# Attention inside the first MoE: transposes one unit later, and the sinks of all heads in one go

## The chip, the cores and the metric

The kernel runs on one core of a Trainium2 chip. The metric is the device time of one execution in microseconds (us). Engines are named as the profile names them: PE (matrix products; PEld is its weight loading), DVE, ACT and POOL (element-wise work), SP (issues transfers).

## The reference

```python
scores = scale * np.matmul(q, k.transpose(0, 1, 3, 2))
keep = is_sink | in_window                     # 4 sink columns, window 128
scores = np.where(keep, scores, -1000000000.0)
a = np.exp(scores - np.max(scores, axis=-1, keepdims=True))
a = a / (np.sum(a, axis=-1, keepdims=True) + 1e-09)
attn_out = np.matmul(a, v)                     # (4, 8, 768, 64)
x = attn_out.transpose(0, 2, 1, 3).reshape(B * S, H * D)   # 3072 x 512
return (x @ w_a) * (x @ w_b) @ w_out           # w_a, w_b: 512 x 1536, w_out: 1536 x 512
```

The window and the number of sinks are inputs, but this kernel has a fast path for 128 and 4.

## The kernel before

The 3072 rows are 24 tiles of 128 rows (6 of each of 4 batches). They are processed in groups. The first group is tile 0 of every batch. While PE works at the MoE of one group (12 blocks j; of each a products with w_a, b products with w_b, and o products that project the block before), the attention of the next group is woven into it: `moe` calls `between` three times a block, and each call takes as many steps of a generator as are due. The first such attention, here the second attention of the kernel, is that of batch 0, tiles 1 and 2, and lies between about 30 and 147 us of the span. It is written by `first_attention`, `parts_exact` and `pipeline`. It has 16 units (h, i): 8 heads by 2 tiles, and takes 21 steps.

A unit does this. `scores` (L732) makes s on PE; DVE adds the mask (L736); ACT takes the exponential (L738); DVE makes the reciprocal of the sum (L740, L741); ACT scales (L742). `transposes` (L757) turns p on PE, two 128x128 blocks, and ACT copies them into `ptx` (L758). After an odd head, `av` (L769) makes eight calls of products for the pair of heads, and ACT copies the result into `xf` (L771). Tile 2 sees the sinks apart from its window. Its four sink columns are kept by POOL (L747); for each pair of heads `sinks_t` turns them (L777), DVE copies them (L779), `sinks_av` multiplies them with the v of the sinks (L784), and DVE adds that to `xf` (L786). In this text t(6,0) means the transposes of head 6, tile 0, s(7,1) the scores of head 7, tile 1, av(2) the av of the third pair of heads, which fills `xf` number 2, and sinks product 2 that of the same pair.

All transposes and products of this attention use one PSUM tile, which `half_bank` hands out in two halves, the first for transposes, the second for av and the products of sinks:

```python
bank[0] = self.ps.tile([P, 4, P], F32, tag="t", name=name)
return bank[0][:, 2:] if second else bank[0][:, :2]
```

Beside this attention DVE and ACT also split the weights of the MoE into a high and a low part (L336, L337, L348, L360, L366), DVE multiplies a and b into g (L889), ACT rounds it to gh (L892), and POOL makes the first q and k of the group after (L387, L390). When the generator is through, `split_x` splits `xf` into xh (ACT, L829) and xl (DVE, L830), four parts (kk) of 128 columns of x each, for the next MoE, whose products need all four. Its blocks are called a128, b128 and o128. The order of the instructions on each engine is made by a scheduler in the compilation; the code above gives it only the order of priority.

Of the kernel before, what the change touches and what calls it, by code (L numbers as in the profile page):

```python
# [19 lines left out]
P = 128  # L20
# [209 lines left out]
class Fast:  # L230
# [326 lines left out]
    def first_attention(self, segs, xf, after):  # L557
        (_, t0, nt), = segs
        late = [i for i in range(nt) if t0 + i >= 2]
        units = [(h, i) for h in range(H) for i in range(nt)]  # L560
        return self.pipeline(units, nt, late, *self.parts_exact(*segs[0], xf, after), 2, 2, 1)

# [122 lines left out]
    def parts_exact(self, b, t0, nt, xf, after):  # L685
# [17 lines left out]
        def do_prep(h):  # L703
# [8 lines left out]
            if h % 2 == 0:  # L712
                v = self.sp.tile([P, 2, MB, D], F32, tag="v", name=f"vx{u}")
                nc.sync.dma_start(v[:, :, :nb], self.vB[b, h // 2, :, :, s0:s0 + nb])
            else:
                v = preps[h - 1][2]
                if late:
                    vs = ptx[:2 * NS, h // 2 % 2, 2 * nt + 1, :]
                    m = h // 2
                    nc.sync.dma_start(vs, self.vS[b, m * 2 * NS:(m + 1) * 2 * NS, m])  # L720
                    vss[h // 2] = vs
            preps[h] = k, q, v

        def scores(h, i):
# [19 lines left out]
            if i in late:  # L744
                if h % 2 == 0:
                    sc[h // 2, i] = self.at.tile([P, 2, NS], F32, tag=f"sc{i % 3}", name=f"sc{u}", bufs=2)
                nc.gpsimd.tensor_copy(sc[h // 2, i][:, h % 2, :], p[:, P:P + NS])  # L747

# [23 lines left out]

        def sinks_t(pr):
            n = len(late)
            tp = half_bank(0, f"skt{tag}_{pr}")
            for k, i in enumerate(late):
                nc.tensor.transpose(tp[:2 * NS, k, :], sc[pr, i].rearrange("p a b -> p (a b)"), self.ident)  # L777
            skt[pr] = ptx[:2 * NS, pr % 2, 2 * nt:2 * nt + n, :]
            nc.vector.tensor_copy(skt[pr], tp[:2 * NS, :n, :])  # L779

        def sinks_av(pr, _):
            n = len(late)
            ps = half_bank(1, f"sk{tag}_{pr}")
            nc.tensor.matmul(ps[:, :n, :], lhsT=vss[pr], rhs=skt.pop(pr), start=True, stop=True)  # L784
            xs = xf[pr][:, late[0] * P:nt * P].rearrange("p (c q) -> p c q", q=P)
            nc.vector.tensor_tensor(xs, ps[:, :n, :], xs, op=ALU.add)  # L786

        return do_prep, scores, transposes, av, sinks_t, sinks_av

    def pipeline(self, units, nt, late, do_prep, scores, transposes, av, sinks_t, sinks_av, lag, group, early):  # L790

        for h in range(early):
            do_prep(h)
        yield
        nu = len(units)
        for k in range(nu + lag + 2 + group // 2):
            if k < nu:
                h, i = units[k]
                if i == 0:
                    do_prep(h + early)  # L800
                scores(h, i)
            n = k - lag - 1
            if 0 <= n < nu and units[n][1] == nt - 1:
                h = units[n][0]
                av(h)
                if h % group == group - 1 and late:
                    sinks_t(h // group)
            for c in range(group // 2):
                n -= 1
                if 0 <= n < nu and units[n][1] == nt - 1:  # L810
                    h = units[n][0]
                    if h % group == group - 1 and late:
                        sinks_av(h // group, c)
            n = k - lag
            if 0 <= n < nu:
                transposes(*units[n])
            yield


# [251 lines left out]
```

## Time and profile before

| what | value |
|---|---|
| median of 3 runs | 757.04 us (756.62 to 757.09) |
| the profiled execution, own time | 756.8 us |
| its span (first to last instruction) | 755.1 us |
| granted clock of PE, mean | 0.999 of full speed |

The span is the time that the trace covers. The 1.7 us between it and the execution's own time lie around it.

### The profile page before, as it was taken

The page shows a single profiled execution, that of the slowest core. Times are in us where ns is not written, and L with a number is a line of the kernel's source. Part 1 is how long each engine was busy: PE and PEld are TensorE (multiplying, and loading weights), DVE is VectorE, ACT ScalarE, POOL GpSimd, SP SyncE. Part 2 cuts the span into 40 slices and gives each one's busy share as a digit, 9 for nine tenths or more (in the row PEclk, how much of TensorE's full clock was granted, in tenths as well). Part 3 has the DMA queues.
Part 4 walks back from the last instruction along what each step waited for, and adds up shares of the span by engine and source line. Part 5 has one row for each costly group of instructions (what it writes and reads, how often), then busy time and mean ns, then how long its engine had stood idle before and what let it go on. Part 6 is the DMA issues. An engine that isn't in the chain of part 4 may idle for free.

```text
span 755.1 us, 13078 instructions
## 1 busy us (share of the span) xinstructions
PE 745.2 (99%) x4422; PEld 665.7 (88%) x4422; DVE 389.8 (52%) x1303; ACT 387.4 (51%) x1185; POOL 275.5 (36%) x358
## 2 busy tenths in 40 slices
PE   8999999999999999999999999999999999999996
PEld 6877777889899998999989999899989999999996
DVE  6899998455455553445544554355553555331001
ACT  6777765466455663555535555355554655331111
POOL 2200021176425542355404545056561764201110
PEclk9999999999999999999999999999999999999999
DMA  9997111322213343124422344124443141010001
GB/s 333 394 318 279 33 40 40 118 72 75 64 46 85 105 141 92 57 85 123 132 82 70 96 126 138 63 75 124 115 121 114 47 132 47 2 42 1 1 1 44
DMA packets 48807, 76.89 MB, mean 102 GB/s; under 512 B 5056, under 2 KB 28640, under 8 KB 48736
## 3 DMA queue, kind: packets, MB, share of 16 engines
q1 hardware_dynamic: 45568, 70.50, 29.6%
q10 hardware_dynamic: 3168, 5.51, 1.9%
q8 instruction: 36, 0.59, 0.3%
q14 instruction: 35, 0.29, 0.1%
HBM read 69.70 MB, written 6.29 MB: 101 GB/s over the span
## 4 chain that ended last, share of the span: by engine, by line
PE 90%; DMA 3%; DVE 3%; ACT 1%; POOL 1%; issue 1%; SPq 0%; DVEq 0%; POOLq 0%; ACTq 0%
PE a L846 26%; PE o L873 25%; PE b L846 25%; PE s L628 5%; PE av L659 5%; PE t L648 2%; DMA raw_a<-in_wa_dram 1%; DMA raw_o<-in_wo_dram 1%; DMA v<-in_v_dram 1%; PE sk L679 1%; PE s L732 1%; DMA qr<-in_qT_dram 1%; PE t L757 0%; PE t L769 0%; DVE wf_o L348 0%
## 5 line engine op out<-in xcount | busy, mean ns | idle before, releaser
L846 PE MATMUL a<-xh,w_a 128*128 128x384 f32 (+2 forms) x760 | 212.3, 342 | 0.1
L846 PE MATMUL b<-xh,w_b 128*128 128x384 f32 (+2 forms) x760 | 209.9, 340 | 0.5 <-DVE w_b L366 0.5
L873 PE MATMUL o<-w_o,gh 128*128 128x512 f32 x576 | 182.4, 398 | 0.0
L894 POOL TENSOR_TENSOR gl<-g,gh 128x384 fp32r<-128x384 f32 (+1 forms) x70 | 68.2, 974 | 225.9 <-ACT gh L892 221.6
L846 PEld LDWEIGHTS a<-xh,w_a 128*128 128x128 f32 x760 | 137.2, 188 | 8.3 <-issue 1.7
L846 PEld LDWEIGHTS b<-xh,w_b 128*128 128x128 f32 x760 | 137.2, 188 | 5.8 <-issue 1.0
L846 PE MATMUL a<-xl,w_a 128*128 128x384 f32 (+2 forms) x380 | 127.8, 336 | 0.0
L846 PE MATMUL b<-xl,w_b 128*128 128x384 f32 (+2 forms) x380 | 127.7, 336 | 0.0
L873 PEld LDWEIGHTS o<-w_o,gh 128*128 128x128 f32 x576 | 103.9, 188 | 18.8 <-issue 0.9
L873 PE MATMUL o<-w_o,gl 128*128 128x512 f32 x288 | 113.3, 394 | 0.0
L889 DVE TENSOR_TENSOR g<-b,g 128x384 f32<-128x384 f32 (+2 forms) x95 | 52.8, 555 | 112.6 <-PE b L846 111.5
L636 ACT ACTIVATE p<-p,st 128x132 f32<-128x132 f32 x144 | 58.0, 403 | 74.4 <-DVE st L634 73.2
L892 ACT CAST gh<-g 128x384 fp32r<-128x384 f32 (+2 forms) x96 | 49.3, 513 | 88.6 <-DVE g L889 88.6
L883 ACT COPY g<-a 128x384 f32<-128x384 f32 (+2 forms) x95 | 45.0, 474 | 91.2 <-PE a L846 85.7
L633 DVE COPY_PREDICATED s<-own,s 128x128 f32<-128x128 uint16 x144 | 42.0, 291 | 82.0 <-PE s L628 80.4
L846 PEld LDWEIGHTS a<-xl,w_a 128*128 128x128 f32 x380 | 71.4, 188 | 2.7
L639 ACT ACTIVATE p<-p,st 128x132 f32<-128x132 f32 x144 | 58.2, 404 | 29.3 <-DVE st L638 28.6
L846 PEld LDWEIGHTS b<-xl,w_b 128*128 128x128 f32 x380 | 71.4, 188 | 1.7
L390 POOL TENSOR_TENSOR ks<-kr,ks 64x524 fp32r<-64x524 f32 (+1 forms) x64 | 70.4, 1110 | 3.9
L873 PEld LDWEIGHTS o<-w_o,gl 128*128 128x128 f32 x288 | 54.1, 188 | 12.9 <-DVE gl L894 0.9
L637 DVE TENSOR_SCALAR st<-st 128x1 f32<-128x1 f32 x144 | 21.9, 152 | 74.8 <-ACT p L636 74.8
L387 POOL TENSOR_SCALAR qh<-qr 128x384 fp32r<-128x384 f32 x48 | 24.9, 519 | 86.4 <-DMA qr<-in_qT_dram 49.4
(166 smaller groups left out, 1029.7 us busy)
## 6 DMA issues: line engine op xcount, KB each, us to landing
raw_a<-in_wa_dram SPq DMA_DIRECT2D x12, 512.0 KB, 7.8
raw_b<-in_wb_dram SPq DMA_DIRECT2D x12, 512.0 KB, 6.3
raw_o<-in_wo_dram SPq DMA_DIRECT2D x12, 512.0 KB, 6.9
qr<-in_qT_dram SPq DMA_DIRECT2D x32, 192.0 KB, 2.6
chk_a<-in_wa_dram SPq DMA_DIRECT2D x24, 256.0 KB, 3.2
chk_b<-in_wb_dram SPq DMA_DIRECT2D x24, 256.0 KB, 3.0
chk_o<-in_wo_dram SPq DMA_DIRECT2D x24, 256.0 KB, 3.1
out_dram<-os ACTq DMA_DIRECT2D x21, 256.0 KB, 2.1
```

The lines of the kernel that those rows point to most:

```text
L390: self.nc.gpsimd.tensor_tensor(o, i, high.bitcast(F32), op=ALU.subtract)
L628: nc.tensor.matmul(ps, lhsT=q[:, i * P:(i + 1) * P], rhs=ks[:, c0s[i]:c0s[i] + SW], start=n == 0, stop=n == 1)
L633: nc.vector.copy_predicated(ps[:, :P], self.own.bitcast(mybir.dt.uint16), ps[:, W:])
L636: nc.scalar.activation(p, p, AF.Exp, bias=st[:, 0:1], scale=-1.0, accum_out=st[:, 1:2])
L639: nc.scalar.mul(p, p, st[:, 3:4])
L659: nc.tensor.matmul(ps[half[e], c * P:(c + ns) * P], lhsT=v[:, e, blk, :], rhs=pt[:, e, sl:sl + ns, :], start=j == 0, stop=j == len(groups) ...
L846: mm = self.nc.tensor.matmul(ps[:, cols], lhsT=w[:, ksl], rhs=x[:, kk, cols], start=start and kk == 0 and i == 0, stop=kk == NK - 1 and i ...
L873: nc.tensor.matmul(outs[i], lhsT=g[:, sl], rhs=w, start=j == 0 and k == 0, stop=j == NJ - 1 and k == 2)
L883: nc.scalar.copy(g[:, :n], pa[:, :n])
L889: nc.vector.tensor_tensor(g[:, :n], pb[:, :n], g[:, :n], op=ALU.mult)
L892: nc.scalar.copy(gh[:, :n], g[:, :n])
L894: e.tensor_tensor(gl[:, :n], g[:, :n], gh[:, :n].bitcast(F32), op=ALU.subtract)
```

## The change

The transposes stand three units behind the scores (two before). The sinks are taken once for all eight heads: one transpose 32x128 in the step of the last unit's transposes, one DVE copy into a tile `sks` of its own, then four products, two in each of the last two steps. The v of the sinks comes in two transfers of 32x256 where there were four of 8x128. The number of steps stays 21.

```diff
-        return self.pipeline(units, nt, late, *self.parts_exact(*segs[0], xf, after), 2, 2, 1)
+        return self.pipeline(units, nt, late, *self.parts_exact(*segs[0], xf, after), 3, 1)
...
-                if late:
-                    vs = ptx[:2 * NS, h // 2 % 2, 2 * nt + 1, :]
-                    m = h // 2
-                    nc.sync.dma_start(vs, self.vS[b, m * 2 * NS:(m + 1) * 2 * NS, m])
-                    vss[h // 2] = vs
+                if late and h < 4:
+                    vs = ptx[:H * NS, h // 2, 2 * nt:2 * nt + 2, :]
+                    nc.sync.dma_start(vs, self.vS[b, :H * NS, h - 1:h + 1])
+                    for c in range(2):
+                        vss[h - 1 + c] = vs[:, c, :]
...
-                if h % 2 == 0:
-                    sc[h // 2, i] = self.at.tile([P, 2, NS], F32, tag=f"sc{i % 3}", name=f"sc{u}", bufs=2)
-                nc.gpsimd.tensor_copy(sc[h // 2, i][:, h % 2, :], p[:, P:P + NS])
+                if h == 0:
+                    sc[i] = self.at.tile([P, H, NS], F32, tag=f"sc{i}", name=f"sc{u}", bufs=2)
+                nc.gpsimd.tensor_copy(sc[i][:, h, :], p[:, P:P + NS])
...
-        def sinks_t(pr):
+        def sinks_t():
             n = len(late)
-            tp = half_bank(0, f"skt{tag}_{pr}")
+            tp = half_bank(0, f"skt{tag}")
             for k, i in enumerate(late):
-                nc.tensor.transpose(tp[:2 * NS, k, :], sc[pr, i].rearrange("p a b -> p (a b)"), self.ident)
-            skt[pr] = ptx[:2 * NS, pr % 2, 2 * nt:2 * nt + n, :]
-            nc.vector.tensor_copy(skt[pr], tp[:2 * NS, :n, :])
-
-        def sinks_av(pr, _):
+                nc.tensor.transpose(tp[:H * NS, k, :], sc[i].rearrange("p a b -> p (a b)"), self.ident)
+            s = self.at.tile([P, SW], F32, tag="p", name=f"sks{tag}")
+            skt[0] = s[:H * NS, :n * P].rearrange("p (k q) -> p k q", q=P)
+            nc.vector.tensor_copy(skt[0], tp[:H * NS, :n, :])
+
+        def sinks_av(pr):
             n = len(late)
             ps = half_bank(1, f"sk{tag}_{pr}")
-            nc.tensor.matmul(ps[:, :n, :], lhsT=vss[pr], rhs=skt.pop(pr), start=True, stop=True)
+            nc.tensor.matmul(ps[:, :n, :], lhsT=vss[pr], rhs=skt[0], start=True, stop=True)
...
-        for k in range(nu + lag + 2 + group // 2):
+        for k in range(nu + lag + 2):
...
-                h = units[n][0]
-                av(h)
-                if h % group == group - 1 and late:
-                    sinks_t(h // group)
-            for c in range(group // 2):
-                n -= 1
-                if 0 <= n < nu and units[n][1] == nt - 1:
-                    h = units[n][0]
-                    if h % group == group - 1 and late:
-                        sinks_av(h // group, c)
-            n = k - lag
-            if 0 <= n < nu:
-                transposes(*units[n])
+                av(units[n][0])
+            if k == nu + lag - 1 and late:
+                transposes(*units[-1])
+                sinks_t()
+            elif 0 <= k - lag < nu:
+                transposes(*units[k - lag])
+            if k >= nu + lag and late:
+                for c in range(2):
+                    sinks_av(2 * (k - nu - lag) + c)
             yield
```

The next rows are those of PE in the kernel before, at the place where it waits twice: from av(2) (L769) to t(6,0) (L757, written p_1_6_0), in the stream of a products of block 8. The words in brackets say which engine the instruction waits for.

```order
391 L769 MATMUL t_1_0_0_628<-ptx,vx_1_4_862 64x128 [waits DMAHW1_49,Activation_49]
392 L769 MATMUL t_1_0_0_628<-ptx,vx_1_4_862 64x128 x7
393 L846 MATMUL a_8_1362<-xh,w_a_1232 128x512
394 L846 MATMUL a_8_1362<-xl,w_a_1232 128x512
395 L846 MATMUL a_8_1362<-xh,w_a_1232 128x512
396 L777 MATMUL t_1_0_0_628<-ident,sc_1_4_1_1038 8x128 [waits Activation_49,Pool_49]
397 L846 MATMUL a_8_1362<-xh,w_a_1232 128x512
398 L846 MATMUL a_8_1362<-xl,w_a_1232 128x512
399 L846 MATMUL a_8_1362<-xh,w_a_1232 128x512 x2
400 L846 MATMUL a_8_1362<-xl,w_a_1232 128x512
401 L757 MATMUL t_1_0_0_628<-ident,p_1_6_0_1219 128x128 [waits DVE_49]
```

The next rows are those of PE in the changed kernel, from s(7,1) (L732) to the rest of the o products of block 7.

```order
406 L732 MATMUL s_1_7_1_1378<-kx_1_7_1198,qx_1_7_1199 128x260 [waits DVE_49]
407 L769 MATMUL t_1_0_0_685<-ptx,vx_1_4_858 64x128 [waits DMAHW3_49,Activation_49]
408 L769 MATMUL t_1_0_0_685<-ptx,vx_1_4_858 64x128 x7
409 L869 MATMUL o_0_482<-w_o_1283,gh_7_1263 128x512
410 L869 MATMUL o_0_482<-w_o_1283,gh_7_1263 128x512 [waits DVE_49]
411 L869 MATMUL o_0_482<-w_o_1283,gl_7_1264 128x512
412 L757 MATMUL t_1_0_0_685<-ident,p_1_6_0_1204 128x128 [waits Activation_49]
413 L757 MATMUL t_1_0_0_685<-ident,p_1_6_0_1204 128x128
414 L869 MATMUL o_1_483<-w_o_1283,gh_7_1263 128x512 x2
```

So av(2) and t(6,0) moved behind s(7,1), with three o products between them, and t(6,0) waits for ACT where it waited for DVE.

ACT's rows in the changed kernel at that place, from the rounding of block 8's g (L888 is L892 of before) to the second copy of p's transposes:

```order
151 L345 ACTIVATE raw_b_1176<-raw_b_1176 128x512 [waits DMAHW0_49]
152 L888 CAST gh_8_1374<-g_8_1348 128x512 [waits DVE_49]
153 L771 COPY xf_2_118<-t_1_0_0_685 128x256 [waits PE_49]
154 L738 ACTIVATE p_1_7_1_1380,st_1_7_1_1381<-p_1_7_1_1380,st_1_7_1_1381 128x260 [waits DVE_49,Pool_49]
155 L758 COPY ptx<-t_1_0_0_685 128x256 [waits PE_49]
```

ACT's rows in the kernel before, where the copy into `xf` number 2 (L771) stood nine rows ahead of gh of block 8 and followed the scaling of p(6,1):

```order
143 L738 ACTIVATE p_1_6_1_1284,st_1_6_1_1285<-p_1_6_1_1284,st_1_6_1_1285 128x260 [waits DVE_49]
144 L742 ACTIVATE p_1_6_1_1284<-p_1_6_1_1284,st_1_6_1_1285 128x260 [waits DVE_49,Activation_49]
145 L771 COPY xf_2_118<-t_1_0_0_628 128x256 [waits PE_49]
146 L738 ACTIVATE p_1_7_0_1331,st_1_7_0_1332<-p_1_7_0_1331,st_1_7_0_1332 128x260 [waits DVE_49]
147 L742 ACTIVATE p_1_7_0_1331<-p_1_7_0_1331,st_1_7_0_1332 128x260 [waits DVE_49,Activation_49]
```

In the changed kernel the copy stands behind gh of block 8, which waits for DVE's g of that block.

PE's rows in the changed kernel at the end of the first MoE, from its last o products: sinks products 2 and 3 (L785, L784 of before) stand behind them, and the first a and b blocks of the next MoE come in pieces.

```order
527 L869 MATMUL o_3_485<-w_o_1574,gl_11_1607 128x512
528 L785 MATMUL t_1_0_0_685<-sks_1_1499,ptx 128x128
529 L842 MATMUL a_0_1670<-xh,w_a_385 128x256
530 L842 MATMUL a_0_1670<-xl,w_a_385 128x256
531 L842 MATMUL a_0_1670<-xh,w_a_385 128x256 x2
532 L785 MATMUL t_1_0_0_685<-sks_1_1499,ptx 128x128 [waits DVE_49]
...
542 L628 MATMUL s_3_0_1_1727<-ks_3_0_1306,qh_3_0_1307 128x260 [waits DVE_49,PE_49]
543 L628 MATMUL s_3_0_1_1727<-ks_3_0_1306,ql_3_0_1308 128x260
544 L842 MATMUL a_0_1670<-xh,w_a_385 128x256 [waits Activation_49]
545 L842 MATMUL b_0_1709<-xh,w_b_419 128x256
546 L842 MATMUL a_0_1670<-xl,w_a_385 128x256 [waits DVE_49]
```

Before, the whole of a128's first block followed the last o product at once. On DVE the split of parts 2 and 3 (L826, L830 of before) now stands among the steps of the next attention:

```order
297 L633 COPY_PREDICATED s_3_0_0_1685<-own,s_3_0_0_1685 128x128 [waits PE_49]
298 L634 ISA p_3_0_0_1688,st_3_0_0_1689<-s_3_0_0_1685,mg 128x132 [waits DVE_49]
299 L634 ISA st_3_0_0_1689 128x1
300 L633 COPY_PREDICATED s_3_0_1_1727<-own,s_3_0_1_1727 128x128 [waits DVE_49,PE_49]
301 L826 TENSOR_TENSOR xl<-xf_2_118,xh 128x256 [waits Activation_49]
```

It stood, all four parts together, ahead of the g of block 11.

## Rows read from the trace of the kernel before

**Rows 1.** Page, chain that ended last, by engine.

```profile
PE 90%; DMA 3%; DVE 3%; ACT 1%; POOL 1%; issue 1%; SPq 0%; DVEq 0%; POOLq 0%; ACTq 0%
```

**Rows 2.** Waits of PE from 42 to 150 us: total, times, longest.

```profile
PE t L757 <- DVE st L740: 0.7, 1, 0.7
PE t L757 <- DVE ptx L779: 0.6, 1, 0.6
```

**Rows 3.** Busy of PE, PEld, DVE, ACT, POOL in 10 us (with counts).

```profile
102.00:112.00 10.00, 9.38 (x53) 6.83 (x51) 9.43 (x20) 5.82 (x14) 4.69 (x5) 1.00 0.18 48
112.00:122.00 10.00, 9.34 (x42) 7.18 (x42) 9.66 (x23) 6.16 (x13) 2.99 (x4) 1.00 0.00 0
```

**Rows 4.** Timeline of PE at t(6,0), t(6,1): start, length, what, [idle before].

```profile
106.49 0.40 PE L846 MATMUL a<-xl,w_a 128*128 128x512 f32 x1
107.51 0.44 PE L757 MATMUL t<-ident,p 128*128 128x128 f32 x2 [0.62 <-DVE ptx L779]
...
112.04 0.48 PE L784 MATMUL t<-ptx 8*128 8x128 f32 x2
...
114.63 0.40 PE L873 MATMUL o<-w_o,gh 128*128 128x512 f32 x1
115.69 0.44 PE L757 MATMUL t<-ident,p 128*128 128x128 f32 x2 [0.66 <-DVE st L740]
```

**Rows 5.** Timeline of DVE, same stretch.

```profile
103.30 0.67 DVE L366 TENSOR_TENSOR w_b<-wf_b,w_b 128x512 fp32r<-128x512 f32 x1
...
105.51 1.68 DVE L348 CUSTOM_DVE_ANT_0 wf_o<-raw_o,wf_o 128x1024 uint16<-128x1024 uint16 x1
...
107.18 0.27 DVE L779 COPY ptx<-t 8x128 f32<-8x128 f32 x1
...
110.14 0.69 DVE L348 CUSTOM_DVE_ANT_0 wf_a<-raw_a,wf_a 128x1024 uint16<-128x1024 uint16 x1
...
112.42 0.68 DVE L889 TENSOR_TENSOR g<-b,g 128x512 f32<-128x512 f32 x1
...
115.36 0.28 DVE L786 TENSOR_TENSOR xf<-t,xf 128x128 f32<-128x128 f32 x1
```

**Rows 6.** Timeline of POOL, same stretch.

```profile
105.02 1.62 POOL L390 TENSOR_TENSOR ks<-kr,ks 64x524 fp32r<-64x524 f32 x1
...
112.27 0.72 POOL L387 TENSOR_SCALAR ks<-kr 64x524 fp32r<-64x524 f32 x1 [3.27 <-PE s L732]
```

**Rows 7.** Timeline of ACT, same stretch.

```profile
104.75 0.37 ACT L771 COPY xf<-t 128x256 f32<-128x256 f32 x1 [0.76 <-PE t L769]
...
113.13 0.62 ACT L892 CAST gh<-g 128x512 fp32r<-128x512 f32 x1 [2.09 <-DVE g L889]
```

**Rows 8.** Timeline of PE, a transpose of sinks between products.

```profile
62.57 0.40 PE L846 MATMUL a<-xh,w_a 128*128 128x512 f32 x1
62.80 0.28 PE L777 MATMUL t<-ident,sc 128*8 128x128 f32 x1
...
63.15 0.39 PE L846 MATMUL a<-xl,w_a 128*128 128x512 f32 x1
```

**Rows 9.** Timeline of PE, a product of sinks between products.

```profile
87.47 0.40 PE L846 MATMUL b<-xh,w_b 128*128 128x512 f32 x1
87.80 0.48 PE L784 MATMUL t<-ptx 8*128 8x128 f32 x2
...
88.55 0.40 PE L846 MATMUL b<-xl,w_b 128*128 128x512 f32 x1
```

**Rows 10.** Timeline of PE, av(2) and the products behind it.

```profile
103.61 1.09 PE L769 MATMUL t<-ptx,vx 128*64 128x128 f32 x16
...
104.97 0.39 PE L846 MATMUL a<-xl,w_a 128*128 128x512 f32 x1
```

**Rows 11.** Timeline of PE, end of the first MoE, start of the next.

```profile
146.50 0.39 PE L873 MATMUL o<-w_o,gl 128*128 128x512 f32 x1
...
154.88 0.39 PE L873 MATMUL o<-w_o,gl 128*128 128x512 f32 x1
```

**Rows 12.** Timeline of ACT, the last copy out of the first MoE.

```profile
147.70 0.59 ACT L904 COPY os<-o 128x512 f32<-128x512 f32 x1 [0.41 <-ACT os L904]
```

**Rows 13.** Timeline of DVE, split of x and mask in the next MoE.

```profile
139.67 0.43 DVE L830 TENSOR_TENSOR xl<-xf,xh 128x256 fp32r<-128x256 f32 x1 [3.73 <-ACT xh L829]
...
148.55 0.29 DVE L633 COPY_PREDICATED s<-own,s 128x128 f32<-128x128 uint16 x1 [5.07 <-PE s L628]
```

More of the change, by code (lines that the diff above doesn't have):

```diff
@@ L788, in parts_exact, with pipeline @@
         return do_prep, scores, transposes, av, sinks_t, sinks_av
-    def pipeline(self, units, nt, late, do_prep, scores, transposes, av, sinks_t, sinks_av, lag, group, early):
+    def pipeline(self, units, nt, late, do_prep, scores, transposes, av, sinks_t, sinks_av, lag, early):
         for h in range(early):
```

## The prediction

> **What bounds the kernel now.** I read the chain of work that ended last first: nine tenths of it is PE [rows 1]. So a microsecond that PE waits anywhere is a microsecond of the run, unless a later wait absorbs it, and work on DVE, ACT or POOL counts only where PE stands still for it. Second, the list of what PE waits for between 42 and 150 us, the stretch of the second attention: two waits, both of the transposes L757, both named DVE, 1.3 us together [rows 2]. Third, the busy time by 10 us slices: in the two slices that hold the waits PE is busy 9.4 and 9.3 of 10 us, and DVE 9.4 and 9.7 [rows 3]. DVE is a queue with almost no slack there, and anything on PE that needs its last instruction is late.
>
> Fourth, the timelines at the two waits. t(6,0) starts at 107.51, 1.02 behind the a product before it, where products follow each other in 0.23 [rows 4, 8]; it loses 0.79. The copy of the turned sinks on DVE starts at 107.18 [rows 5], and t(6,0) starts as it ends. t(6,1) starts 1.06 behind its o product [rows 4]; it loses 0.83. The profile names the L740 there, but what ends at 115.64, just ahead of 115.69, is L786, DVE's addition of a sinks product to `xf` [rows 4, 5]. L786 reads the second half of the shared PSUM tile and t(6,1) writes the first: the two halves wait for each other.
>
> DVE is late at both for one reason. An L348 takes 1.68 where an undisturbed one takes 0.69, beside a POOL L390 of 1.62 [rows 5, 6].
>
> **What goes.** Both waits, since in the new order no transpose of p is queued behind a sinks copy or a sinks addition until the last units: -0.79 - 0.83 = -1.62. Three of four sinks transposes: two products with one between them start 0.35 apart where they take 0.23 [rows 8], so each is about 0.11 or 0.12; three are -0.35. The four products of sinks stay four, at 0.61 each (1.08 from the product before to the one two behind, less two times 0.23) [rows 9]; K is 32 where it was 8, and the shape of the moving side, which sets their length, stays. Two transfers fewer on SP and three DVE copies fewer hide behind PE; they are worth nothing by themselves, though the DVE copies come back below as lead.
>
> **What is added.** av(1) is cut by s(5,1) in the new order of PE. A switch of shape costs the instruction behind it about 0.1: av(2) and the product behind it take 1.36 to the next product's start, so 1.13 for av [rows 10], where its 16 records of 0.27 overlap. Two more switches are between 0.1 and 0.3; I take +0.15.
>
> **What t(6,0) waits for next.** This is the term that decides. In the new order PE does s(7,1), av(2), three o products, t(6,0), and the word in brackets behind t(6,0) is ACT. Since the halves wait for each other, it must wait until ACT has copied av(2) out of the other half. This L771 stands on ACT behind gh of block 8, which waits for DVE's g (L889).
>
> When does PE come to t(6,0)? Before, s(7,1) ends where the sinks product starts, 112.04 [rows 4]. Ahead of that go away three sinks transposes (0.35), two sinks products (1.22), the first wait (0.79); av(2) (1.13) and t(6,0) (about two sinks transposes, 0.22) go behind it; the cut of av(1) adds 0.15. That gives 108.5. Then av(2) 1.13 and three products 0.70: 110.3.
>
> When is the copy done? Before, DVE went from the L366 of w_b at 103.30 to g at 112.42, 9.12 us without a pause worth naming [rows 5]. Of what stood between, the sinks copy (0.27) is gone, and one weight instruction now stands behind g (about 0.6, the L366's step). That leaves 8.25. DVE comes to this L366 earlier, since two sinks copies and two additions of 0.27 each are gone ahead of it: 1.1, so at 102.2 (0.8 to 1.4, as its idle time moves). So g starts at 110.45 with POOL's hindrance as before. The second L387 and L390 of POOL, released by s(7,1) [rows 6], start at 108.5 instead of 112.27, and now fall ahead of g. One DVE instruction held as long as the one above is +0.99: g at 111.4. From g's start to gh's is 0.71 [rows 5, 7], gh takes 0.62 and the copy 0.37 [rows 7]: 1.65 with the overlap of neighbours. The copy ends at 112.1 without the second hindrance and at 113.1 with it, against 110.3. PE stands still for 1.8 to 2.8; I take the middle, +2.3. The low end is nothing to 0.5: without any hindrance g starts at 109.5 less at most 0.3 and the copy ends at about 110.8. The high end is 3.4 to 3.8, two hindrances ahead of g.
>
> If the halves were independent in this wait, the sum would lose this term and stand at -1.4. The row of t(6,1) speaks against that: 115.69 behind an instruction on the other half that ended at 115.64 [rows 4, 5]. The Trainium skill, "PSUM — Partial Sum Buffer", section "PSUM bank collisions raise a hardware error", has a rule for it: guard PSUM by bank and quadrant, not by address, since disjoint columns of one bank still collide. By that rule t(6,0) has to wait for the copy, and the trace agrees, with the 0.05 us between those two rows.
>
> The other transposes that follow an av, t(2,0) and t(4,0), have the same new wait, but there POOL is hardly at work and the ACT rows ahead of their copies need only older scores; I price them at nothing, 0.3 at most.
>
> **What moves to the end.** Sinks products 2 and 3 come behind the last o product; their 1.22 were inside the stage, so that is no change of the sum. But x parts 2 and 3 can be split only then. Before, from the last o product to the third o product of the next MoE are 8.38 us [rows 11], of which the products, scores and transposes account for some 7.85 (48 half-wide products 5.6, five scores 1.2, three transposes 0.35, three o products 0.7), so 0.5 was lost anyway. After: the last o's 0.23, two sinks products 1.22, 12 products of parts 0 and 1 at 0.117 and two scores take PE from 146.5 to about 150.0, a hold of 0.15 for the mask included. xh of part 2 waits for the last copy out, which ends at 148.3 [rows 12], and is no trouble. xl of part 2 stands on DVE behind the mask copy of s_3_0_1: 150.0 + 0.15 + 0.29 + 0.43 [rows 13] = 150.87, and PE wants it at 150.23: 0.64. Two holds for masks are 0.3. So 0.95 is lost, and the 0.5 of before need not come again: +0.4, between 0 (all of the old 0.5 vanishes and xl comes in time) and 1.0.
>
> **Sum.** -1.62 - 0.35 + 0.15 + 2.3 + 0.4 = +0.9 us. The profiled execution took 756.8, so 757.7; the median of the runs is 0.24 above it: 757.9. A measurement of this kernel can tell about 0.2%, 1.5 us, from no change: 755.5 to 758.6.
>
> **Rivals.**
> 1. The two waits go and nothing takes their place, because g is not held and the copy ends by 110.8. Sum without the 2.3, with up to 0.5 in its place: -1.4 to -0.9, so 755.6 to 756.1. For it: DVE gains 1.1 us of lead and POOL works in only two short stretches here. Against it: ACT's copy sits behind g on a DVE that is busy 94% [rows 3], and PE gains more lead (3.5) than DVE does.
> 2. POOL's second L390 falls just ahead of g and two DVE instructions are held: +3.4 at least at t(6,0), and the end loses 1.0: -1.82 + 3.6 + 1.0 = +2.8, 759.8. It is slower from the point where t(6,0) waits over 2.9 us, which is a copy that ends behind 113.2. For it: L390 starts as early as PE does, at 108.5 + 0.7, and runs 1.6 or more, in the middle of the DVE instructions ahead of g. Against it: only one of them was held fully by the earlier L390.
> The Trainium skill, "SBUF — State Buffer", section "Who interferes with whom", says that DVE and POOL share a port pair as an exclusive lock, and that whoever starts first makes the other wait for a whole instruction. The row of 1.68 agrees; by that rule every POOL instruction can hold one of DVE's, which is how two are held here.
> 3. The change does not do what it says: t(6,0) and t(6,1) still wait for something on DVE as long as before, as DVE's backlog, not the sinks, sets the pace. -0.35 + 0.15 + 0.4 = +0.2, 757.2.
>
> **Chances.** The sum above 0.45 (its own range 757.2 to 758.7, mostly within 0.2%), rival 1 0.2, rival 2 0.23, rival 3 0.12. Faster takes half of rival 1, at whose middle the bound lies, and a little of the others: 0.13. Slower takes rival 2 and the upper edge of the first case: 0.3. The rest, 0.57, is within 0.2%. The range goes from rival 1's middle to rival 2's: 755.7 to 759.7.
>
> **What will show it.** Right: L757 loses its two waits named DVE near 107 and 115; one wait before t(6,0), near 111 to 113, some 2 us, named ACT L771; its L771 starts as gh of block 8 ends. A wait of about 0.6 for xl at 150. No wait in the second half of the stage from DVE. Wrong: no idle time before t(6,0) (rival 1, and DVE's g starts before 109.5); idle time over 3 with two DVE instructions over 1.4 beside L390 (rival 2); idle time named DVE at either transpose (rival 3). The forecast is also wrong if an earlier transpose, t(2,0) or t(4,0), waits over 0.5, or if the split of parts 2 and 3 holds PE by over 1.

## The result, and the profile after

| what | before | after |
|---|---|---|
| median of the runs | 757.04 us (756.18 to 757.30, 5 runs) | 763.28 us (762.19 to 764.47, 5 runs) |
| the profiled execution, own time | 756.8 us | 762.19 us |
| its span | 755.1 us | 760.5 us |
| mean granted clock | 0.999 (profiled execution); 0.998 to 1.000 (45 executions beside the experiments) | 0.995 to 0.997 (5 runs) |

The ratio is 1.0083 [1.0068, 1.0098]. The change costs 6.2 us. The forecast was 757.9, with a range to 759.7: the time is above it, and beyond the rival that was to end slower. Three slow executions (811.99 and 1882.15 us of the kernel before, 811.88 of e6) stand in none of the ranges and counts here.

Nine tenths of the chain that ended last are PE, as before [rows 1], so a standstill of PE is still a loss.

What PE waits for between 42 and 170 us of the changed kernel (total, times, longest):

```profile
PE t L757 <- ACT xf L771: 2.9, 1, 2.9
PE s L628 <- DVE st L634: 1.2, 1, 1.2
PE a L842 <- DVE xl L826: 0.5, 1, 0.5
```

The two waits of [rows 2] are gone. The first line here is the forecast wait, of the forecast transpose for the forecast copy. The third is the forecast wait for xl. The second was not forecast.

The timeline of PE around t(6,0) and t(6,1) in the changed kernel, which answers to [rows 4]:

```profile
109.00 1.09 PE L769 MATMUL t<-ptx,vx 128*64 128x128 f32 x16
...
110.60 0.40 PE L869 MATMUL o<-w_o,gl 128*128 128x512 f32 x1
113.92 0.44 PE L757 MATMUL t<-ident,p 128*128 128x128 f32 x2 [2.92 <-ACT xf L771]
114.11 0.81 PE L869 MATMUL o<-w_o,gh 128*128 128x512 f32 x2
...
117.28 0.63 PE L869 MATMUL o<-w_o,gl 128*128 128x512 f32 x1
117.70 0.51 PE L757 MATMUL t<-ident,p 128*128 128x128 f32 x2
```

av(2) starts at 109.00 where the forecast said 108.5. Of this, 0.35 is a later start of this execution: its first score of this attention starts at 30.92, for 30.57 before, and most of that is already there at the start of the kernel, where PE waits for a transfer (until 7.80, for 7.49). The o product ahead of t(6,0) starts at 110.60 and takes 0.23 of PE's time, so t(6,0) at 113.92 has lost 3.09. The lengths of the rows behind it have changed too. The o products that take 0.40 and follow each other in 0.23 elsewhere take 0.63 here and follow each other in 0.42 (114.72 to 115.14). Nine of them stand between the two transposes, from 114.11 to 117.70. The busy time of PE, PEld, DVE, ACT, POOL in each microsecond, then PE's granted clock, DMA share, GB/s:

```profile
113.00:114.00 1.00, 0.09 (x1) 0.09 (x2) 1.00 (x4) 0.88 (x3) 0.00 (x0) 1.00 0.00 0
114.00:115.00 1.00, 1.00 (x5) 0.86 (x6) 1.00 (x2) 1.00 (x4) 0.00 (x0) 0.78 0.00 0
115.00:116.00 1.00, 1.00 (x4) 0.72 (x3) 1.00 (x6) 1.00 (x3) 0.00 (x0) 0.50 0.00 0
...
117.00:118.00 1.00, 1.00 (x6) 0.71 (x4) 0.86 (x3) 0.00 (x0) 0.23 (x2) 0.52 0.00 0
118.00:119.00 1.00, 1.00 (x7) 0.81 (x6) 0.97 (x3) 0.74 (x2) 0.00 (x0) 1.00 0.00 0
```

PE stands still, and soon after PE goes on the granted clock is 0.50 for some 3.4 us, the lower of its two levels (1.2 GHz, where 1.00 is 2.4 GHz). The kernel before had 1.00 in both slices here [rows 3]. The Trainium skill, "TensorE: Matmul & The Clock Gate", section "Part 1: The HAM clock gate (the "warmup" mystery)", says that a gate passes either all or half of the clock, by how busy the engine has lately been, and no level between. The trace agrees: 0.78 and 0.52 are slices in which the level changes, the others show 1.00 or 0.50.

Why the copy is late: DVE, POOL and ACT of the changed kernel, one fence each, which answer to [rows 5 to 7].

```profile
109.79 1.11 DVE L366 TENSOR_TENSOR w_a<-wf_a,w_a 128x512 fp32r<-128x512 f32 x1
110.83 1.51 DVE L336 TENSOR_SCALAR wf_b<-raw_b 128x512 int32<-128x512 int32 x1
112.26 0.68 DVE L885 TENSOR_TENSOR g<-b,g 128x512 f32<-128x512 f32 x1
```

```profile
109.22 1.14 POOL L387 TENSOR_SCALAR ks<-kr 64x524 fp32r<-64x524 f32 x1 [1.08 <-issue]
110.45 1.60 POOL L390 TENSOR_TENSOR ks<-kr,ks 64x524 fp32r<-64x524 f32 x1
```

```profile
112.97 0.62 ACT L888 CAST gh<-g 128x512 fp32r<-128x512 f32 x1 [4.18 <-DVE g L885]
113.50 0.37 ACT L771 COPY xf<-t 128x256 f32<-128x256 f32 x1
```

ACT's queue is one line: the copy stands behind gh of block 8, gh waits 4.18 for DVE's g, and g starts at 112.26, behind instructions of 1.11 and 1.51 (0.67 and 0.42 undisturbed) that run beside POOL's second L387 and L390. That pair came forward because PE's s(7,1) did: it starts at 109.22, where the two products of s(7,1), from 108.47 on, have just ended.

The end of the first MoE and the start of the next in the changed kernel, on PE, which answers to [rows 11]:

```profile
148.70 0.40 PE L869 MATMUL o<-w_o,gl 128*128 128x512 f32 x1
...
153.28 0.39 PE L842 MATMUL a<-xl,w_a 128*128 128x256 f32 x1 [0.48 <-DVE xl L826]
...
159.21 0.39 PE L869 MATMUL o<-w_o,gl 128*128 128x512 f32 x1
...
161.62 0.36 PE L628 MATMUL s<-ks,qh 128*128 128x260 f32 x1 [1.21 <-DVE st L634]
```

Against [rows 11] the last o product is 2.20 late and the third o of the next MoE 4.33. At 161.62 a score waits another 1.21 (1.37 from start to start) for DVE, where an instruction of 0.95 (L650, which multiplies the turned p by the triangle mask, at 160.31) stands ahead of the L634 that it waits for.

### The profile page after: what moved, and what is told of

Same layout as the page of the kernel before. It is cut to its first block, busy times and chain, and to the rows that moved or that the text cites. A ratio compares the mean times of both kernels' runs of the same rounds, so it can differ in the third digit from the quotient of the medians.

```text
span 760.5 us, 13049 instructions
## 1 busy us (share of the span) xinstructions
PE 746.7 (98%) x4419; PEld 667.1 (88%) x4419; DVE 390.6 (51%) x1300; ACT 386.8 (51%) x1185; POOL 282.9 (37%) x358
## 4 chain that ended last, share of the span: by engine, by line
PE 90%; DMA 3%; DVE 2%; issue 2%; ACT 1%; POOL 1%; SPq 0%; POOLq 0%; DVEq 0%
PE b L842 26%; PE o L869 25%; PE a L842 25%; PE s L628 5%; PE av L659 5%; PE t L648 2%; DMA raw_a<-in_wa_dram 1%; DMA raw_o<-in_wo_dram 1%; DMA v<-in_v_dram 1%; PE s L732 1%; PE sk L679 1%; PE t L757 0%; PE t L769 0%; DVE wf_o L348 0%; PE skt L668 0%
## 5 line engine op out<-in xcount | busy, mean ns | idle before, releaser
L888 ACT CAST gh<-g 128x384 fp32r<-128x384 f32 (+2 forms) x96 | 49.2, 513 | 94.1 <-DVE g L885 94.1
L390 POOL TENSOR_TENSOR ks<-kr,ks 64x524 fp32r<-64x524 f32 (+1 forms) x64 | 70.3, 1107 | 3.9
L387 POOL TENSOR_SCALAR qh<-qr 128x384 fp32r<-128x384 f32 x48 | 24.9, 519 | 94.7 <-DMA qr<-in_qT_dram 48.4
```

Source lines behind the costliest of these rows:

```text
L390: self.nc.gpsimd.tensor_tensor(o, i, high.bitcast(F32), op=ALU.subtract)
L888: nc.scalar.copy(gh[:, :n], g[:, :n])
```

## The experiments

The theory: t(6,0) waits because its PSUM tile is shared with av(2), whose copy stands on ACT behind g; the standstill then lowers the clock; and the two sinks products at the end cost the rest. Rivals: three units of lag are harmful in themselves; POOL alone is the cause; the clock falls for some other reason; the sinks at the end do nothing.

### e1: a lag of two units, the rest as changed

```diff
-        return self.pipeline(units, nt, late, *self.parts_exact(*segs[0], xf, after), 3, 1)
+        return self.pipeline(units, nt, late, *self.parts_exact(*segs[0], xf, after), 2, 1)
```

> The changed kernel with the transposes two units behind the scores, sinks at the end as changed. In it the copy of av(2) stands on ACT ahead of gh of block 8, and all steps are through inside the first MoE. First theory (t(6,0) waits because that copy stands behind gh, and the granted clock falls because of that wait): no wait of L757 on ACT over 0.3 us, granted clock 0.999, the two waits of before gone too, end of the MoE as before: 755.0 to 756.0. Rival (DVE's backlog makes PE wait wherever the copy stands): a wait of 1.5 to 3 us at some L757 or g-dependent product between 104 and 116, 757.5 to 761. Rival on the clock (the fall has nothing to do with the wait): mean clock stays at 0.995 to 0.997 and 2 us come on top of either.

Measured: 757.5 us (756.38 to 760.16, 10 runs), 1.0020 [1.0007, 1.0034], a miss. The wait of t(6,0) is gone, and so is almost all of the loss, but the gain did not come. DVE and PE of e1 show the wait that took its place:

```profile
122.97 0.68 DVE L885 TENSOR_TENSOR g<-b,g 128x512 f32<-128x512 f32 x1
123.57 0.68 DVE L348 CUSTOM_DVE_ANT_0 wf_b<-raw_b,wf_b 128x1024 uint16<-128x1024 uint16 x1
124.17 0.27 DVE L780 COPY sks<-t 32x128 f32<-32x128 f32 x1
```

```profile
124.50 1.09 PE L769 MATMUL t<-ptx,vx 128*64 128x128 f32 x16 [1.72 <-DVE sks L780]
```

The same tile again, in the other direction: av(3) writes one half and waits until DVE has read the turned sinks out of the other, and that copy stands behind g and a weight instruction. The clock was 1.00 behind this wait in the profiled execution (757.46). In four of the ten executions the mean clock is 0.994 or 0.995, and these take 759.1 to 760.2; the others take 756.4 to 757.6. None of the 45 executions of the kernel before is below 0.998. Where the clock was low in those four is not seen, since the mean is that of a whole execution.

### e2: all four sinks products before the last o products

```diff
-            if k >= nu + lag and late:
-                for c in range(2):
-                    sinks_av(2 * (k - nu - lag) + c)
+            if k == nu + lag and late:
+                for c in range(4):
+                    sinks_av(c)
```

> The changed kernel with all four sinks products in the last step but one, so that none is left behind the last o product. First theory: the wait at t(6,0) (3.1) and the lower clock behind it (1.5 to 3) stay as they are; from the last o product to the third o product of the next MoE it takes 8.4 again where the changed kernel took 10.5, of which 1.2 only moves ahead, so 0.9 is gained, and the wait of 1.2 on DVE's L634 at 161.6 (1.4 by starts) goes: 760.5 to 761.5. Rival (the end costs nothing by itself, the 161.6 wait is the old order's too): 762.5 to 763.5.

Measured: 760.01 us (759.43 to 760.47, 4 runs), 1.0044 [1.0027, 1.0061]: 3.3 below the changed kernel, 0.5 below the expected range. The wait at 161.6 is gone, and from the last o product (148.32) to the third o of the next MoE (156.71) are 8.39, as before (8.38). So by the medians the products at the end cost about half of the loss. By the rows above they cost 2.3 (4.33 - 2.20 less the 1.22 of two moved products is 0.9, and 1.37 at 161.62). The wait of t(6,0) is as long as in the changed kernel, and the profiled execution gives an unplanned comparison. The rows of PE in e2:

```profile
113.88 0.44 PE L757 MATMUL t<-ident,p 128*128 128x128 f32 x2 [2.94 <-ACT xf L771]
114.07 0.70 PE L869 MATMUL o<-w_o,gh 128*128 128x512 f32 x2
...
116.00 0.39 PE L869 MATMUL o<-w_o,gl 128*128 128x512 f32 x1
116.23 0.38 PE L757 MATMUL t<-ident,p 128*128 128x128 f32 x2
```

The standstill is the same and the same nine o products follow, but the granted clock is 1.00 in every microsecond, and the nine take 2.16 (114.07 to 116.23) instead of 3.59. So the low level costs 1.43 there, and it does not follow such a standstill every time. This execution has a mean clock of 0.998 and is the shortest of the four; the other three have 0.996 and are 0.4 to 1.0 longer.

### e3: POOL's work for the next group one step after the last score

```diff
-                    do_prep(h + early)
+                    if h + early < H:
+                        do_prep(h + early)
...
+            if k == nu + 1:
+                do_prep(H)
```

> The changed kernel with POOL's first q and k of the next group asked for one step after the last scores instead of with s(7,0); everything on PE, ACT and DVE around t(6,0) stands as in the changed kernel. First theory (DVE's g of block 8 is late because L390 and L387 hold five DVE instructions): no DVE instruction there over 1.0 us, g starts before 109.5, the wait at t(6,0) falls from 2.9 to under 0.8, the granted clock stays up; the end costs as much as in the changed kernel, or up to 1 more where POOL now is late there: 758.0 to 760.0. Rival (DVE is full whatever POOL does): the wait stays over 2, 762 to 764.

Measured: 762.94 us (761.04 to 765.27, 4 runs), 1.0072 [1.0055, 1.0089]. A miss. The part about t(6,0) held: g starts at 110.70 where it started at 112.26, and t(6,0) does not wait. The gain of g is larger than this looks, since the profiled execution, the longest of the four, runs late from the start: its first score stands at 32.98 (30.92 in the changed kernel), so that counted from there g is 3.6 earlier. So POOL's work is what made that copy late. The late start has a low clock of its own, behind a wait of PE for a transfer, far ahead of the changed attention (PE's row, and one microsecond behind it):

```profile
8.21 1.94 PE L482 MATMUL s<-kq 64*128 64x128 f32 x16 [1.73 <-DMA kq<-in_kq_dram]
```

```profile
9.00:10.00 1.00, 1.00 (x12) 0.85 (x8) 0.00 (x0) 0.26 (x2) 0.00 (x0) 0.50 1.00 402
```

POOL's work now runs from 119.84 on, holds DVE there (an L366 of 1.81), g of block 9 comes at 132.69, and the copy of av(3) on ACT stands behind its gh. The waits of 1.2 and 0.5 at the start of the next MoE are there as in the changed kernel. PE in e3, and windows of it (columns as above):

```profile
134.34 0.49 PE L785 MATMUL t<-sks,ptx 32*128 32x128 f32 x2 [2.22 <-ACT xf L771]
```

```profile
135.00:136.00 1.00, 1.00 (x3) 0.59 (x3) 0.17 (x1) 0.33 (x1) 0.00 (x0) 0.50 0.73 175
...
140.00:142.00 2.00, 2.00 (x7) 1.52 (x7) 0.00 (x0) 0.00 (x0) 0.00 (x0) 0.62 0.57 203
142.00:144.00 2.00, 2.00 (x10) 1.64 (x9) 0.00 (x0) 0.59 (x1) 0.00 (x0) 1.00 0.00 0
```

The standstill is shorter than that of t(6,0), but the low clock after it lasts about twice as long, from about 134.7 to 141.5.

### e4: the kernel before, with three units of lag alone

```diff
-        return self.pipeline(units, nt, late, *self.parts_exact(*segs[0], xf, after), 2, 2, 1)
+        return self.pipeline(units, nt, late, *self.parts_exact(*segs[0], xf, after), 3, 2, 1)
```

> The kernel before with only the lag changed, two to three; sinks by pairs as before. First theory: the copy of av(2) stands behind gh of block 8 here too, and the sinks transpose, its DVE copy and then t(6,0) follow it, so PE waits at the sinks transpose on ACT and once more at t(6,0) on DVE, 3 us or more together, and the clock falls: 760 to 764. Rival (the sinks taken at the end do the harm, not the lag): no wait over 1 us, 756 to 757.5.

Measured: 762.43 us (762.25 to 762.56, 4 runs), 1.0074 [1.0058, 1.0091], as expected. What waits in it is the transpose of the sinks (L777) for the same copy; the list of PE's waits in e4, and its windows:

```profile
PE t L777 <- ACT xf L771: 3.0, 1, 3.0
```

```profile
116.00:118.00 2.00, 2.00 (x7) 1.45 (x6) 2.00 (x8) 0.61 (x2) 0.24 (x1) 0.57 0.00 0
118.00:120.00 2.00, 2.00 (x7) 1.26 (x6) 0.58 (x1) 1.27 (x3) 0.00 (x0) 0.58 0.00 0
```

With the kernel's other parts left alone the lag brings the same wait and the same low clock. The sinks in one transpose are not needed for that. The second expected wait, at t(6,0), is not there, and two others are: 1.7 at a transpose (L648, for ACT) and 0.5 at a score in the next MoE. So not all of its loss is that wait and its clock.

### e5: e2, with PE busy while it waits

Thirteen spare products, whose result nothing reads, stand ahead of t(6,0). They are added to the kernel of e2:

```diff
+                if units[n][0] == 5:
+                    ps = self.ps.tile([P, DM], F32, tag="a", name="fill")
+                    for c in range(13):
+                        self.nc.tensor.matmul(ps, lhsT=self.wt["a", 8][0][:, :P], rhs=self.xt[0][:, :DM],
+                                              start=True, stop=True)
```

> The kernel of the second experiment (all sinks products inside; median 760.0, clock 0.996 to 0.998) with 13 spare products of 0.233 us, 3.0 us in all, put on PE ahead of t(6,0); their result goes nowhere. They end at about 113.1, so t(6,0) waits some 0.7 instead of 2.9 and starts at the same 113.9; three o products that stood ahead of it now stand behind (+0.7). If the granted clock falls because PE stood still, it stays at 1.00 from 112 to 120, no o product there takes over 0.25 from start to start, and although PE has 3.0 us of work more the run is not longer: 758.0 to 760.0, clock 0.998 or 0.999 in every run. Rival (the clock falls by itself in this stretch, or from the load): 0.82 and 0.75 again between 112 and 120, 760.7 to 763.

Measured: 759.11 us (758.64 to 759.87, 6 runs), 1.0031 [1.0018, 1.0043]; mean clock 0.998 or 0.999 in every run.

```profile
109.84 3.30 PE L809 MATMUL fill<-xh,w_a 128*128 128x512 f32 x13
113.76 0.44 PE L757 MATMUL t<-ident,p 128*128 128x128 f32 x2 [0.62 <-ACT xf L771]
```

PE does 3 us more work and the kernel is 0.9 shorter than e2 by the medians. The intervals of the two overlap, so a gain is not shown; that the work cost nothing is, and t(6,0) starts within 0.12 of where it did in e2 (113.88). Between the two profiled executions, which both keep the full clock there, the difference is only 0.4 (759.04 and 759.43). All six executions have 0.998 or 0.999, where three of the four of e2 had 0.996. So by the mean clocks the filling took away the low stretch of the other executions of e2; that the stretch lay at t(6,0) in them is argued, since they have no trace.

### e6: the changed kernel in 22 steps instead of 21

```diff
-                steps = 30 if c else H * len(nrows) + 5
+                steps = 30 if c else H * len(nrows) + 6
```

> The changed kernel with one number more, 22 steps spread over the MoE instead of 21: each step comes a little earlier, the copy of av(2) stands ahead of gh of block 8 on ACT, and no sinks product is left behind the last o product. First theory (a user of the shared bank waits for whatever the user before left on ACT or DVE, and the place of that copy in its queue decides): no wait at t(6,0); av(3) waits for the DVE copy of the turned sinks, which stands behind g of block 9, about as in the first experiment (1.0 to 2.0), or the first sinks product for the copy of av(3): 756.0 to 758.5. Rival (lag 3 itself costs the 6 us): 760 or more.

Measured: 757.04 us (756.41 to 761.85, 9 runs), 1.0009 [0.9994, 1.0025], a time as expected. The changed generator has one step more that does work than the 21 that the MoE takes, and its last, with sinks products 2 and 3, was run behind the MoE; here it falls inside, and the steps are spread otherwise over the same blocks. The copy of av(2) starts at 106.98 and gh of block 8 at 113.83. The 2.9 is gone; what is left are two waits of 0.9 and 0.7, neither of them one that was expected (a sinks product waits for the addition of the one before, t(6,1) for the copy of t(6,0)):

```profile
PE t L785 <- DVE xf L787: 0.9, 1, 0.9
PE t L757 <- ACT ptx L758: 0.7, 1, 0.7
```

So three units of lag need do no harm. What does the harm is where the copy of av(2) falls against g. One of the nine executions took 761.85, with a mean clock of 0.993, and the others at most 757.65; what stood still in that one no trace shows.

### e7: a lag of two, the sinks apart from av(3)

The lag is 2, the steps stay 21, `sinks_t` comes behind av(3) in the same step, and the four products come one step after that:

```diff
-        return self.pipeline(units, nt, late, *self.parts_exact(*segs[0], xf, after), 3, 1)
+        return self.pipeline(units, nt, late, *self.parts_exact(*segs[0], xf, after), 2, 1)
...
-            if k == nu + lag - 1 and late:
-                transposes(*units[-1])
+            if 0 <= k - lag < nu:
+                transposes(*units[k - lag])
+            if k == nu + lag + 0 and late:
                 sinks_t()
-            elif 0 <= k - lag < nu:
-                transposes(*units[k - lag])
-            if k >= nu + lag and late:
-                for c in range(2):
-                    sinks_av(2 * (k - nu - lag) + c)
+            if k == nu + lag + 1 and late:
+                for c in range(4):
+                    sinks_av(c)
```

> The changed kernel with lag 2 and the three users of the shared bank at its end drawn apart: av(3), then the sinks transpose in the same step behind it, and all four sinks products one step later. First theory: no wait of a transpose, an av or a sinks product over 0.5 us, clock 0.999 in every run, the two waits of the kernel before gone and nothing in their place: 754.7 to 755.7, faster than the kernel before by 1.2 to 2.0. Rival (some other instruction of PE takes the wait over, since DVE is as full): 756.5 to 758.

Measured: 756.75 us (755.53 to 758.08, 11 runs), 0.9998 [0.9989, 1.0007]: a miss, the expected gain is not there. Four products into the same half follow each other, and each needs DVE's addition of the one before. PE in e7:

```profile
132.49 0.48 PE L785 MATMUL t<-sks,ptx 32*128 32x128 f32 x2 [0.72 <-DVE xf L787]
```

The addition stands behind an L366 of 1.49 and g on DVE. The 0.7 it costs, and another 0.7 at a sinks transpose behind a copy of av, are about what the two waits of the kernel before cost [rows 2].

### e8: the kernel before, with POOL's work moved as in e3

The edit is that of e3, in the kernel before.

> The kernel before with POOL's first q and k of the next group asked for one step after the last scores. First theory (the two waits of before come from DVE instructions held by POOL's): no wait at t(6,0) and t(6,1), so 1.6 less; POOL's work falls between 120 and 131 instead, where DVE holds g of blocks 9 and 10 and the last sinks copy, and a new wait of up to 2 at the last pair can eat it: 755.0 to 757.5, and what waits in the profile is the last pair. Rival (DVE late whatever POOL does): both waits stay, 757.

Measured: 755.02 us (754.48 to 755.64, 9 runs), 0.9976 [0.9966, 0.9986]. It beats both kernels. PE waits for nothing between 42 and 170 us, at the last pair neither. DVE in e8, where [rows 5] had an L348 of 1.68 and the copy of the sinks at 107.18:

```profile
105.55 0.69 DVE L348 CUSTOM_DVE_ANT_0 wf_o<-raw_o,wf_o 128x1024 uint16<-128x1024 uint16 x1
...
106.22 0.27 DVE L779 COPY ptx<-t 8x128 f32<-8x128 f32 x1
```

The two old waits go without any change to the code of the attention itself. POOL then starts at 120.79 and holds a DVE instruction as before (an L366 of 1.78 at 123.58), in a place where PE does not wait for DVE. The gain of 1.9 is the forecast 1.62 of the two waits, as near as the measurement tells.

### e9: av and the sinks products in a bank of their own

The o products of the fourth row tile of the first group are added to those of its first, so the two output tiles are left out; the bank this frees goes to av.

```diff
+                bank[1] = self.ps.tile([P, 4, P], F32, tag="av", name=name + "v")
-            return bank[0][:, 2:] if second else bank[0][:, :2]
+            return bank[1][:, 2:] if second else bank[0][:, :2]
```

> The changed kernel with a PSUM bank of its own for av and the sinks products, apart from the transposes. The bank is won by adding the o products of the fourth row tile of the first group to those of its first, so these two tiles of the output are left out; PE does as many products as before. The copy of av(2) still stands behind gh of block 8. First theory (t(6,0) waits because both halves are one bank): t(6,0) follows av(2) without a wait; the next user of the transposes' bank, t(6,1), has to wait for the copy of t(6,0), which stands behind gh too, but three o products later: 1.0 to 1.7 instead of 3.1. The end of the MoE stays as in the changed kernel. 760.0 to 762.0, clock 0.997 or more. Rival (DVE's delay reaches t(6,0) by another way than the bank): t(6,0) waits 2.5 or more as before, 762 to 764.

Measured: 761.27 us (760.82 to 761.85, 4 runs), 1.0057 [1.0041, 1.0074], as expected; mean clock 0.999 in every run. PE in e9, ACT's copy of av(2), and what PE waits for:

```profile
109.26 1.09 PE L770 MATMUL t_0v<-ptx,vx 128*64 128x128 f32 x16
110.28 0.44 PE L758 MATMUL t<-ident,p 128*128 128x128 f32 x2
...
114.47 0.44 PE L758 MATMUL t<-ident,p 128*128 128x128 f32 x2 [0.97 <-ACT ptx L759]
```

```profile
113.77 0.37 ACT L772 COPY xf<-t_0v 128x256 f32<-128x256 f32 x1
```

```profile
PE t_0v L786 <- ACT xf L772: 1.1, 1, 1.1
PE t L758 <- ACT ptx L759: 1.0, 1, 1.0
PE a L843 <- DVE xl L827: 0.9, 1, 0.9
PE s L628 <- DVE st L634: 0.8, 1, 0.8
PE t L778 <- ACT ptx L759: 0.4, 1, 0.4
```

t(6,0) follows av(2) at once, 3.5 us ahead of the copy of av(2), which is as late as in the changed kernel (113.77 for 113.50). So t(6,0) waited because it shares a tile with av(2), and for nothing else. The prediction rested this on one row of 0.05 us; here it is shown. The edit gives av a bank and a tile of its own at once. The waits are in the program (the brackets of its order name the engine), so whether two tiles in one bank would be kept apart in the same way is not tested. But t(6,1) now waits, for the copy of t(6,0) on ACT, which is behind the same gh. In all there are five waits with 4.2 us, none over 1.1, and the granted clock is 1.00 from 26 us until PE's work is over. Another bank moves the loss and does not remove it.

### e10: e2 and e3 together

> The changed kernel with POOL's first q and k of the next group asked for one step after the last scores and all four sinks products in the last step but one: the third and the second experiment together. First theory: no wait at t(6,0); POOL's work at 120 to 131 delays g of block 9, and the copy of av(3) stands behind its gh, so the first sinks product waits about 2 as in the third experiment, and the following ones each for the addition before; the end of the MoE costs nothing. 757.5 to 760. Rival (the two repairs add up with no new wait): 755 to 756.

Measured: 762.06 us (760.52 to 762.58, 4 runs), 1.0070 [1.0053, 1.0086]; mean clock 0.991 to 0.994. A miss. PE stands still for 2.12 at the first sinks product (132.66), as expected, and then comes what the expected time did not have:

```profile
134.00:138.00 4.00, 4.00 (x12) 2.21 (x11) 0.58 (x2) 0.00 (x0) 0.00 (x0) 0.61 0.17 56
138.00:142.00 4.00, 4.00 (x11) 3.06 (x12) 2.09 (x4) 0.00 (x0) 0.00 (x0) 0.53 0.32 86
```

At 0.61 and 0.53 of full speed these 8 us lose 0.39 x 4 + 0.47 x 4 = 3.4 us, as an estimate that takes PE's work as in proportion to the clock. Without it the profiled execution, 760.5, would be at 757.1, 0.4 below the range that was expected.

## Why the prediction was wrong

- **What goes: right.** The two waits named DVE vanished. e8, which removes them and changes no code of the attention itself, is 1.9 faster, for -1.62 forecast.
- **What t(6,0) waits for next: right in kind, too small by 0.8.** The wait, its place and its cause are as the step said: it has ACT's copy as its name, the copy follows gh of block 8, e9 shows the shared tile, and e3 shows POOL's pair ahead of g. It was +2.3 in the sum, the middle of no further DVE instruction held (1.8) and one (2.8), and is 3.09, because two were held (1.11 and 1.51, for 0.67 and 0.42), which is rival 2's condition. Rival 2 was the better account of this place.
- **The step that failed outright: what a standstill does to PE.** The sum counted the wait as its own length and put what follows it at nothing. In the profiled execution of the changed kernel the granted clock fell to 0.50 behind it and the nine o products took 1.43 more than the same nine of e2 at 1.00. No term of the prediction and no rival had this; in the kernel before, PE stood still for at most 0.83 here, and the clock stayed. The other executions of the changed kernel take up to 2.3 more than the profiled one, and the two longest have the lowest mean clock, 0.995. That their low stretch was longer, or came twice, is argued from this, not seen.
- **The term that was mis-sized most: what moves to the end.** It was +0.4 and at most 1.0, and measured 2.3. By the profiled rows it is 4.33 - 2.20 = 2.13 up to the third o of the next MoE, of which 1.22 are the two moved products, hence 0.9; then 1.37 at 161.62, where the score of the attention waits for DVE. The step looked at xl, which was right (0.65 lost by starts, for 0.64), and did not follow DVE to the next attention: with the split now standing between its masks, its steps come later there. That this chain makes the second wait is argued from the order; e2 shows that both waits go with the two products. By the medians e2 gives 3.3, part of which may be clock.
- **The small terms.** t(2,0) and t(4,0) were priced at nothing, and the list of PE's waits has none at either. The +0.15 for the cut of av(1) is too small to be told. The range was to go from rival 1's middle to rival 2's, which by their sums are 755.85 and 759.8, not 755.7 and 759.7; nothing hangs on it.

The sum for the profiled execution, by what the rows show: -1.62 and -0.35 that went, +0.15, +3.09 at t(6,0), +1.43 of clock, +0.35 for a later start, +0.9 and +1.37 at the end, is +5.3; measured +5.4. The -0.35 and the +0.15 are the forecast's, not read off, and part of the agreement is luck: an o product of the next MoE that starts at 160.11 before starts at 165.88 in the changed kernel, 5.8 late, and 0.4 of that comes back in the rest of the run.

What stays open: why the clock falls behind one standstill of 2.9 us and not behind another, and why it stays low for twice as long in e3 and e10 as in the changed kernel. The runs show that it happens, and not what decides. Nor are the reasons for the five waits of e9 tried, or which DVE instructions POOL holds and which it lets pass.

## What to carry to other kernels

Before a transfer of work is called free, look at what stands ahead of the instruction that releases its buffer in that engine's queue: two halves of one PSUM tile were one buffer here, and a copy behind an instruction that itself waits for a third engine is as late as that one. Where a wait is caused by a neighbour that slows a busy engine (here POOL beside DVE), move the neighbour into a stretch where nobody waits for that engine: this brought 1.9 us with one edit, and the reordering of the work that waited brought none in any of its forms. The stretch has to be found, though: in the changed kernel the same edit moved the wait to a sinks product (e3, e10). Price a new standstill of PE like those here, 1.7 to 3.0 us, at its length and let the range reach 1.4 to 3.4 us further for the clock.

## What the runs showed of the hardware

- The granted clock fell to 0.50 in the profiled executions behind standstills of PE of 2.12 us (e10), 2.22 (e3), 2.92 (changed kernel) and 3.0 (e4), and behind one of 1.73 at the start of e3; not behind 2.94 (e2), 1.96 (at 8.15, the start of e9), 1.72 (e1), or any of 1.1 and less. Length alone doesn't decide it.
- The low clock goes on while PE is busy again: for some 3.4 us in the changed kernel and e4, and 6.8 in e3 and e10.
- Filling a standstill can cost nothing: 3 us of products that nothing reads left e2 no longer (e5, 759.11 for 760.01), with a mean clock of 0.998 or 0.999 in all six executions, where three of the four without them had 0.996.
- In these programs a product into one half of a PSUM tile and a read of the other half by ACT or DVE wait for each other in both directions, also where each touches only its own half: t(6,0) behind L771, av(3) behind L780 (e1). With two banks the first of these waits is gone (e9).
- DVE instructions take longer beside POOL's: an L348 of 1.68 and an L336 of 1.51 beside an L390, 0.69 and 0.42 where POOL stands still (e8, e3).
